# Attention opening: which engine squares and copies the second unit, and when GpSimd starts

## The chip, the cores and the metric

The kernel runs on one core of a Trainium2 chip. A core has five engines that run side by side, each with its own in-order list of instructions: PE (TensorE, matmuls), DVE (VectorE), ACT (ScalarE), POOL (GpSimd) and SP (SyncE, which here only issues DMAs). They meet through semaphores. The metric is the device time of one launch in microseconds (us), a median over runs. A profile of one execution gives the span from the first to the last instruction, each instruction's start and duration, and the PE clock that was granted.

## What is computed

Attention with root-mean-square-normalised queries and keys, and behind it a two-layer network with a leaky ReLU. q, k, v have the shape (8, 12, 448, 64): batch, heads, sequence, head dimension.

```python
def rmsnorm(x, g):
    rms = np.sqrt(np.mean(x * x, axis=-1, keepdims=True) + 1e-06)
    return x / rms * g
q_n, k_n = rmsnorm(q, g_q), rmsnorm(k, g_k)
scores = np.matmul(q_n, k_n.transpose(0, 1, 3, 2)) / np.sqrt(64)
scores = scores - np.max(scores, axis=-1, keepdims=True)
attn = np.exp(scores)
attn = attn / (np.sum(attn, axis=-1, keepdims=True) + 1e-09)
x = np.matmul(attn, v).transpose(0, 2, 1, 3).reshape(3584, 768)
h = x @ w_in                      # (768, 2048)
out = np.maximum(0.01 * h, h) @ w_out
```

## The kernel before

**Units.** The 96 heads are worked off as 24 units of four heads (three units to a batch element). A unit's q and k each lie in a tile of 128 partitions x 896 fp32 numbers: 2 pairs of heads x 7 sequence groups x 64.

**Preparation of a unit u** takes these steps, each a helper of the kernel. `load(u)` issues two DMAs on SP's queue, q and k, into a ring of three buffers, so a load waits until the unit three before has been normalised. Squares: `prep_sq` on ScalarE or `prep_sqp` on GpSimd, into tiles that share a ring of three buffers. `prep_ssq` adds up each row's 64 squares on VectorE. `prep_rinv` forms 1/rms on ScalarE with a logarithm and an exponential on a few numbers. `prep_norm` multiplies q and k by it on VectorE and writes fp16 (`n16`). `prep_tr` (through `trn` for units 1 to 3) transposes 128 x 128 blocks on PE into PSUM, and `vcopy` (VectorE) or `acopy` (ScalarE) copies them out as `qkT`; q's copy multiplies by the weights g.

**A unit's attention.** There are seven key steps t. `qk` computes a step's scores into one of two PSUM slots, `ex` takes their exponential on ScalarE into `et` (fp16). Before the first exponential one bound for the unit has to be known: `shift_max` takes the maximum of step 0 on VectorE and forms the diagonal `dg`, `shift_mm` spreads it over the partitions with one matmul, and VectorE turns it into the bias `eb`. `close(u)` sums up the exponentials on PE (`zsum_slot`), starts the next unit's exponential and second score step, multiplies with v (`pv`), and forms 1/sum on ScalarE (`zinv`: a logarithm and an exponential over 128 x 896). `xmul` multiplies the two on VectorE. `score0(u)` is a unit's score step 0 computed ahead, in two auxiliary PSUM banks.

**The order.** Under `tc.manual_schedule()` (line 576) each engine executes its instructions in the order in which the program calls the helpers. Lines 577 to 628 open unit 0, lines 650 to 681 are unit 0's seven steps with the preparation of units 1 and 2 between them, lines 683 to 708 unit 1, lines 710 to 746 unit 2, and from line 748 a loop runs over units 3 to 23; there a queue of matmul groups of the network is spread over the attention steps by a list of costs.

**GpSimd** has its own list: make constants, squares of unit 1's q (line 599), two v loads (600, 601), squares of unit 1's k (619), `gate(0)` (620), the first half of `w_in` as four DMAs (621), unit 2's squares (622), v of unit 2 (626). `gate(u)` copies one number of `n16`: it makes GpSimd, and all that is queued behind it there, wait until unit u's keys are normalised. `feed(u)` (line 629) is the loads, gate, squares and v of later units.

**Unit 0's keys** are handled in two parts: K0 is group 0, K1 groups 1 to 6; `trk` (line 608) transposes and copies a part. `warm(n, bank)` issues n matmuls of 128 x 128 whose results are not used.

The lines that fix the order around the change, before:

```python
        prep_norm(0, K0, (1,))
        tpk = aux([P, NS, P], FP16, "tp")
...
        trk(K0, vcopy)
        prep_norm(0, K1, (1,))
        qk(0, STEPS[0])
        shift_max(0)
        trk(K1, acopy)
```

Of the kernel before, what the change touches and what calls it, by code (L numbers as in the profile page):

```python
# [18 lines left out]
def kernel(  # L19
# [35 lines left out]
    def aux(shape, dtype, name):  # L55
        return psum.tile(shape, dtype, tag="aux", bufs=4, name=name)
# [30 lines left out]
    def load_w_in(n0, n):  # L87
        for a in range(2):
            for r in range(2):
                nc.gpsimd.dma_start(win16[64 * a:64 * a + 64, :, r, n0:n0 + n], win_v[a, :, :, r, n0:n0 + n])  # L90
# [7 lines left out]
    st = {}  # L98

    def rows(x, u):  # L100
        b, g = divmod(u, NQ)
        return x[b, QH * g:QH * g + QH].rearrange("(a r) (p t) d -> (r p) a (t d)", r=2, t=NS)

    def load(u, engines=None):
        raw[u] = [raws.tile([P, 2, NS, D], FP32, tag=name, name=name) for name in ("rq", "rk")]
        st[u] = {}
        for t, src, eng in zip(raw[u], (q, k), engines or (nc.sync, nc.sync)):
            eng.dma_start(t.rearrange("p a t d -> p a (t d)"), rows(src, u))

    def load_v(u):  # L110
        nc.gpsimd.dma_start(vts[u % NV].rearrange("p a t d -> p a (t d)"), rows(v, u))  # L111

    ALL = (0, NS)
# [7 lines left out]
    def buf(u, name):  # L121
        if name not in st[u]:
            shape, dtype, bufs = SHAPES[name]
            st[u][name] = prep_p.tile(shape, dtype, tag=name[:2] if bufs == 3 and name != "qkT" else name, bufs=bufs, name=name)
        return st[u][name]
# [3 lines left out]
    def prep_sq(u, c=ALL, tis=BOTH):  # L129
        for ti in tis:  # L130
            nc.scalar.activation(buf(u, f"sq{ti}")[:, :, c[0]:c[1]], raw[u][ti][:, :, c[0]:c[1]], AF.Square)  # L131

    def prep_sqp(u, tis=BOTH):
        for ti in tis:
            nc.gpsimd.tensor_tensor(buf(u, f"sq{ti}"), raw[u][ti], raw[u][ti], op=ALU.mult)
# [4 lines left out]
    def prep_ssq(u, c=ALL, tis=BOTH):  # L140
        for ti in tis:
            nc.vector.tensor_reduce(buf(u, "ssq")[:, ti, :, c[0]:c[1]], buf(u, f"sq{ti}")[:, :, c[0]:c[1]],  # L142
                                    axis=AXL.X, op=ALU.add)

    def prep_rinv(u, tis=BOTH):
        x = slice(tis[0], tis[-1] + 1)
        nc.scalar.activation(buf(u, "uu")[:, x], buf(u, "ssq")[:, x], AF.Ln, bias=eps_t, scale=1.0 / D)
        nc.scalar.activation(buf(u, "rinv")[:, x], buf(u, "uu")[:, x], AF.Exp, bias=0.0, scale=-0.5)  # L148

    def prep_norm(u, c=ALL, tis=BOTH):  # L150
        n = c[1] - c[0]
        for ti in tis:
            src = raw[u][ti]
            nc.vector.tensor_tensor(  # L154
                buf(u, "n16")[:, ti, c[0]:c[1]].rearrange("p s a d -> p a s d"), src[:, :, c[0]:c[1]],
                buf(u, "rinv")[:, ti, :, c[0]:c[1], None].broadcast_to([P, 2, n, D]), op=ALU.mult)

    def prep_tr(u, ti, copies):
        tp = aux([P, NS, P], FP16, "tp")
        for (lo, hi), copy in copies:  # L160
            for x in range(lo, hi):
                nc.tensor.transpose(tp[:, x, :], buf(u, "n16")[:, ti, x].rearrange("p a d -> p (a d)"), ident16)
            copy(buf(u, "qkT")[:, ti, lo:hi], tp[:, lo:hi], ti == 0)
# [12 lines left out]
    def slot():  # L176
        return psum.tile([P, 2, 512], FP32, tag="sT", bufs=2, name="sT")

    def score(u, t, banks):
        for r in range(2):  # L180
            for a in range(2):
                nc.tensor.matmul(banks[a][64 * r:64 * r + 64, 0:S].rearrange("p (t x) -> p t x", t=NS),  # L182
                                 kT(u, r, a, t), qT(u, r, a), start=True, stop=True)

    def qk(u, steps):
        st[u]["sT"] = []
        for t in steps:
            sT = slot()
            score(u, t, (sT[:, 0], sT[:, 1]))
            st[u]["sT"].append((t, sT))  # L190

    def ex(u):
        s = st[u]
        if "et" not in s:
            s["et"] = epool.tile([P, NS, 2, S], FP16, tag="et", name="et")
        for t, sT in s["sT"]:
            if isinstance(sT, list):
                for a in range(2):
                    nc.scalar.activation(s["et"][:, t, a], sT[a][:, 0:S], AF.Exp, bias=s["eb"], scale=1.0)
            else:  # L200
                nc.scalar.activation(s["et"][:, t], sT[:, :, 0:S], AF.Exp, bias=s["eb"], scale=1.0)  # L201
# [21 lines left out]
    def shift_bank(u):  # L223
        st[u]["pb"] = aux([P, 512], FP32, "pb")

    def shift_mm(u):
        s = st[u]
        if u > 0 and "pslot" in st[u - 1]:
            pb = st[u - 1]["pslot"][:, :, S:S + 64]
            for x in range(2):  # L230
                nc.tensor.matmul(pb[:, x], onesp, s["dg"][:, 64 * x:64 * x + 64], start=True, stop=True)
            nc.vector.tensor_reduce(s["spare"][:, 510:511], pb, axis=AXL.XY, op=ALU.max)  # L232
        else:
            if "pb" not in s:
                shift_bank(u)
            pb = s["pb"]
            nc.tensor.matmul(pb[:, 0:P], onesp, s["dg"], start=True, stop=True)
            nc.vector.tensor_reduce(s["spare"][:, 510:511], pb[:, 0:P], axis=AXL.X, op=ALU.max)
        s["eb"] = small.tile([P, 1], FP32, tag="eb", name="eb")
        nc.vector.tensor_scalar(s["eb"], s["spare"][:, 510:511], -1.0, DELTA, op0=ALU.mult, op1=ALU.add)  # L240

    def gate(u):
        nc.gpsimd.tensor_copy(gate_t, buf(u, "n16")[:, 1, NS - 1, 1, D - 1:D])
# [11 lines left out]
    def zsum_slot(u):  # L255
        s = st[u]
        s["zslot"] = slot()
        s["zt"] = [s["zslot"][:, r] for r in range(2)]
        zsum(u)
# [59 lines left out]
    def pv(u, t0=0, t1=NS):  # L319
        s = st[u]  # L320
        if t0 == 0 and "pslot" not in s:
            s["pv"] = [aux([P, 512], FP32, "pv") for r in range(2)]
        for t in range(t0, t1):
            for r in range(2):
                for a in range(2):
                    nc.tensor.matmul(s["pv"][r][64 * a:64 * a + 64, 0:S], vts[u % NV][64 * r:64 * r + 64, a, t],  # L326
                                     s["et"][64 * r:64 * r + 64, t, a], start=(t == 0), stop=(t == NS - 1))
# [241 lines left out]
    K0, K1 = (0, 1), (1, NS)  # L569
    VV = ((ALL, vcopy),)  # L570

    def warm(n, bank):
        for x in range(n):
            nc.tensor.matmul(bank[:, P:2 * P], onesp, onesp, start=True, stop=True)

    with tc.manual_schedule():
# [19 lines left out]
        nc.vector.tensor_copy(gcol, gps[:, 0:1])  # L596
        prep_ssq(0, ALL, (1,))
        prep_rinv(0, (1,))
        prep_sqp(1, (0,))
        load_v(0)  # L600
        load_v(1)
        prep_norm(0, CA, (0,))
        prep_norm(0, CB, (0,))
        prep_tr(0, 0, ((CA, acopy), (CB, acopy)))
        prep_norm(0, K0, (1,))
        tpk = aux([P, NS, P], FP16, "tp")

        def trk(c, copy):
            for x in range(*c):
                nc.tensor.transpose(tpk[:, x, :], buf(0, "n16")[:, 1, x].rearrange("p a d -> p (a d)"), ident16)  # L610
            copy(buf(0, "qkT")[:, 1, c[0]:c[1]], tpk[:, c[0]:c[1]])

        trk(K0, vcopy)
        prep_norm(0, K1, (1,))
        qk(0, STEPS[0])
        shift_max(0)
        trk(K1, acopy)
        load(3)
        prep_sqp(1, (1,))
        gate(0)  # L620
        load_w_in(0, 1024)
        prep_sqp(2)
        shift_bank(0)
        warm(12, st[0]["pb"])
        shift_mm(0)
        load_v(2)
        prep_ssq(1, ALL, (0,))

        def feed(u):
            load(u + 4)  # L630
# [4 lines left out]
        def trn(u, ti, copy):  # L635
            prep_tr(u, ti, ((ALL, copy),))
# [5 lines left out]
        def close(u):  # L642
            n = u + 1
            zsum_slot(u)
            ex(n)
            qk(n, (1,))
            pv(u)
            zinv(u)

        ex(0)  # L650
        prep_ssq(1, ALL, (1,))
        prep_rinv(1)
        prep_norm(1)
        prep_ssq(2)
        feed(0)
        load_w_in(1024, 1024)
        wb = aux([P, 512], FP32, "warm")
        qk(0, (1,))
        ex(0)
        warm(16, wb)  # L660
        qk(0, (2,))
        ex(0)
        warm(12, wb)
        qk(0, (3,))
        ex(0)
        warm(6, wb)
        qk(0, (4,))
        ex(0)
        trn(1, 0, vcopy)
        trn(1, 1, acopy)  # L670
        qk(0, (5,))
        ex(0)
        qk(0, (6,))
        ex(0)
        prep_rinv(2)
        score0(1)
        shift_max(1)
        shift_bank(1)
        warm(20, st[1]["pb"])
        shift_mm(1)  # L680
        close(0)

        prep_norm(2)
        prep_ssq(3)
# [163 lines left out]
```

The softmax here doesn't subtract the row's maximum and nothing guards it: scores larger than these inputs give would overflow.

## Time and profile before

| what | value |
|---|---|
| median of 3 runs (lowest to highest) | 432.72 us (432.71 to 432.97) |
| span of the profiled execution | 431.2 us |
| mean granted PE clock | 0.990 |
| HBM read and written | 45.61 MB, 11.01 MB |
| unit 1's exponentials start | 28.07 us |
| unit 2's exponentials start | 36.99 us |
| unit 3's first exponential | 49.20 us |

The profiled execution is one more execution of the same program; only its span is known, and what lies before its first and after its last instruction is not in it. Busy times are per engine and can overlap. In a timeline row the first number is the start in us from the beginning of the span, the second the duration; a row with xN stands for N instructions in a row, and the bracket says how long the engine had been idle and which work ended that. Instructions of one engine can overlap by about 0.1 us, as the next one is fed while the last one writes its results. What matters for this change lies in the first 50 us.

### The profile page before, as it was taken

Reading aid. Unit: us, or ns where it says so; the run is one execution under the profiler, and the core shown is the slowest. Engines: PE = TensorE matmul, PEld = TensorE weight load, DVE = VectorE, ACT = ScalarE, POOL = GpSimd, SP = SyncE. Lnnn points to the kernel's source line nnn. Section 1 sums busy time; section 2 is a strip of 40 time slices with the busy share of each in tenths; the row PEclk is TensorE's granted clock in tenths of the full one; section 3 lists DMA queues with packets and bytes.
Section 4 is the critical chain, followed back from the end, with each engine's and each line's share of the span. In section 5 each row is a group of like instructions: output and inputs, shape, how many; then the busy total and the mean of one; then the engine's idle time right before and its main releaser. Section 6 shows DMA issues by size and latency. Waiting matters only on the chain.

```text
span 431.2 us, 8844 instructions
## 1 busy us (share of the span) xinstructions
PE 409.3 (95%) x3645; PEld 211.2 (49%) x3645; DVE 273.2 (63%) x434; ACT 306.5 (71%) x466; POOL 86.6 (20%) x77
## 2 busy tenths in 40 slices
PE   7677999999989999999999999999999999999996
PEld 6545444445444544454445544454445444455553
DVE  5898656888659865487369864587359840542162
ACT  5389888757986779966986789966986757643400
POOL 2885423300002102112102102111101101010000
PEclk9699999999999999999999999999999999999999
DMA  8999993789566896578555797488572460212013
GB/s 264 198 239 252 237 254 85 143 170 221 154 104 114 194 206 161 143 128 212 156 103 136 170 209 171 130 141 194 160 109 44 118 143 16 44 38 73 2 44 103
DMA packets 66476, 62.37 MB, mean 145 GB/s; under 512 B 35716, under 2 KB 61572, under 8 KB 66436
## 3 DMA queue, kind: packets, MB, share of 16 engines
q1 hardware_dynamic: 55840, 49.62, 46.7%
q0 software_dynamic: 10272, 11.80, 17.8%
q8 instruction: 28, 0.46, 0.4%
q10 hardware_dynamic: 324, 0.39, 0.3%
q14 instruction: 12, 0.10, 0.1%
HBM read 45.61 MB, written 11.01 MB: 131 GB/s over the span
## 4 chain that ended last, share of the span: by engine, by line
PE 63%; ACT 16%; DVE 12%; issue 3%; ACTq 0%; DVEq 0%
PE hps L347 25%; ACT et L201 8%; PE ma L427 7%; PE md L427 6%; PE sT L182 5%; PE sT L326 4%; PE op L387 4%; PE mc L427 4%; DVE n L154 3%; PE mb L427 3%; ACT gt L341 3%; PE zc L269 3%; DVE ssq L142 1%; DVE sT L219 1%; ACT x L281 1%
## 5 line engine op out<-in xcount | busy, mean ns | idle before, releaser
L201 ACT ACTIVATE et<-sT,eb 128x896 f16<-128x896 f32 x166 | 158.6, 1005 | 15.6 <-PE sT L182 13.3
L347 PE MATMUL hps<-xt,win 128*128 128x448 f16 x756 | 151.0, 353 | 0.2 <-DVE xt L335 0.2
L347 PEld LDWEIGHTS <-win 128*128 128x128 f16 x756 | 70.6, 98 | 71.4 <-issue 9.9
L341 ACT ACTIVATE gt<-hps 128x448 f16<-128x448 f32 x126 | 65.7, 541 | 20.1 <-PE hps L347 19.4
L306 POOL TENSOR_TENSOR xt<-x,rz 128x896 f16<-128x896 f32 x16 | 33.5, 2092 | 150.8 <-DMA rz<-zs 49.8
L154 DVE TENSOR_TENSOR n<-rq,rinv 128x896 f16<-128x896 f32 (+2 forms) x25 | 27.5, 1102 | 48.4 <-ACT rinv L148 44.9
L182 PE MATMUL sT<-qkT 64*64 64x448 f16 x664 | 52.6, 366 | 4.8 <-ACT et L201 4.3
L142 DVE TENSOR_REDUCE ssq<-sq 128x14 f32<-128x896 f32 (+2 forms) x49 | 50.1, 1055 | 1.2 <-ACT sq L131 1.2
L427 PEld LDWEIGHTS <-sa 128*128 128x128 f16 x352 | 32.8, 98 | 26.3 <-issue 6.1
L281 ACT COPY x<-sT 128x896 f32<-128x896 f32 x19 | 17.2, 907 | 39.5 <-DVE sT L232 39.5
L111 POOL DMA_DIRECT2D vt<-in_v_dram x24 | 18.2, 760 | 114.4 <-PE sT L326 106.9
L427 PEld LDWEIGHTS <-gt 128*128 128x128 f16 x264 | 25.2, 98 | 20.3 <-issue 4.4
L219 DVE TENSOR_REDUCE sT<-sT 128x1 f32<-128x896 f32 x22 | 24.0, 1093 | 17.5 <-PE sT L182 17.5
L182 PEld LDWEIGHTS <-qkT 64*64 64x64 f16 x672 | 15.8, 104 | 39.0 <-issue 35.9
L387 PE MATMUL op<-wout,gt 128*128 128x384 f16 x192 | 34.1, 327 | 0.0
L427 PE MATMUL ma<-wout,gt 128*128 128x384 f16 x176 | 32.3, 326 | 0.1
L154 DVE TENSOR_TENSOR n<-rk,rinv 128x896 f16<-128x896 f32 (+2 forms) x25 | 30.1, 1206 | 0.0
L326 PE MATMUL sT<-et,vt 64*64 64x448 f16 x532 | 28.5, 349 | 0.3
L408 DVE TENSOR_TENSOR sa<-gt 128x512 f16<-128x512 f16 (+1 forms) x15 | 8.1, 543 | 29.6 <-ACT gt L341 29.6
L326 PEld LDWEIGHTS <-vt 64*64 64x64 f16 x672 | 20.4, 107 | 10.8 <-issue 1.1
L387 PEld LDWEIGHTS <-gt 128*128 128x128 f16 x192 | 17.7, 98 | 14.0 <-issue 3.2
L453 ACT COPY ost<-ma 128x384 f32<-128x384 f32 x11 | 5.3, 480 | 23.6 <-PE ma L427 23.6
(87 smaller groups left out, 444.9 us busy)
## 6 DMA issues: line engine op xcount, KB each, us to landing
rq<-in_q_dram SPq DMA_DIRECT2D x24, 448.0 KB, 5.0
rk<-in_k_dram SPq DMA_DIRECT2D x24, 448.0 KB, 5.9
out_dram<-ost SPq DMA_DIRECT2D x52, 192.0 KB, 3.8
rz<-zs SPq DMA_DIRECT2D x38, 224.0 KB, 3.3
vt<-in_v_dram POOLq DMA_DIRECT2D x24, 224.0 KB, 5.0
win<-in_moe_w_in_dram POOLq DMA_DIRECT2D x8, 384.0 KB, 9.4
wout<-in_moe_w_out_dram POOLq DMA_DIRECT2D x2, 1536.0 KB, 23.7
out_dram<-ost SPq DMA_DIRECT2D x4, 96.0 KB, 2.1
```

What stands on the lines that cost most here:

```text
L142: nc.vector.tensor_reduce(buf(u, "ssq")[:, ti, :, c[0]:c[1]], buf(u, f"sq{ti}")[:, :, c[0]:c[1]], axis=AXL.X, op=ALU.add)
L154: nc.vector.tensor_tensor(buf(u, "n16")[:, ti, c[0]:c[1]].rearrange("p s a d -> p a s d"), src[:, :, c[0]:c[1]], buf(u, "rinv")[:, ti, :, ...
L182: nc.tensor.matmul(banks[a][64 * r:64 * r + 64, 0:S].rearrange("p (t x) -> p t x", t=NS), kT(u, r, a, t), qT(u, r, a), start=True, stop=True)
L201: nc.scalar.activation(s["et"][:, t], sT[:, :, 0:S], AF.Exp, bias=s["eb"], scale=1.0)
L219: nc.vector.tensor_reduce(s["spare"][:, 511:512], sT[:, :, 0:S], axis=AXL.XY, op=ALU.max)
L281: nc.scalar.copy(s["x32"], s["pslot"][:, :, 0:S])
L306: eng.tensor_tensor(xts[b][:, g], s["x32"], s["rz"], op=ALU.mult)
L326: nc.tensor.matmul(s["pv"][r][64 * a:64 * a + 64, 0:S], vts[u % NV][64 * r:64 * r + 64, a, t], s["et"][64 * r:64 * r + 64, t, a], start=(t ...
L341: nc.scalar.activation(dst, src, AF.Prelu, bias=0.0, scale=1.0, alpha=0.01)
L347: nc.tensor.matmul(hps[:, 0:S], win16[:, kt // 2, kt % 2, ts(ft, P)], xt[:, kt // 2, kt % 2], start=(kt == 0), stop=(kt == KT - 1))
L387: nc.tensor.matmul(op2[:, 0:HC], gt[:, ft, ds(col(t), P)], wout16[:, ft, ds(HC * half, HC)], start=(ft == 0), stop=(ft == FT - 1))
L427: nc.tensor.matmul(bank[:, 0:HC], a[:, f], b[:, f], start=(first and f == 0), stop=(f == HF - 1), skip_group_check=not first)
```

## The change

Unit 1's squares leave GpSimd. ScalarE computes q's after unit 0's query copies and k's after the copy of K1. K1 is normalised right after K0, before K0 is transposed and copied. GpSimd's first work after the constants is `gate(0)`; behind it come v of unit 0, the first half of `w_in`, unit 2's squares, v of unit 1, v of unit 2.

In unit 0's steps, both of unit 1's sums stand behind the first bias. The second score step and its exponential move ahead of unit 1's inverse root, its normalisation and `feed(0)`. Both transposed tiles of unit 1 are copied by VectorE, q after score step 5 and k after step 6. Unit 2's sums move behind the bias of unit 1, and its inverse root behind `close(0)`. The numbers of unused matmuls change: 12 to 8 before the first bias, 6 to 12 after step 3, a new 6 after step 4, 20 to 16 before unit 1's bias.

```diff
         prep_ssq(0, ALL, (1,))
         prep_rinv(0, (1,))
-        prep_sqp(1, (0,))
-        load_v(0)
-        load_v(1)
         prep_norm(0, CA, (0,))
         prep_norm(0, CB, (0,))
         prep_tr(0, 0, ((CA, acopy), (CB, acopy)))
         prep_norm(0, K0, (1,))
+        prep_norm(0, K1, (1,))
+        prep_sq(1, ALL, (0,))
         tpk = aux([P, NS, P], FP16, "tp")
...
         trk(K0, vcopy)
-        prep_norm(0, K1, (1,))
         qk(0, STEPS[0])
         shift_max(0)
         trk(K1, acopy)
+        prep_sq(1, ALL, (1,))
         load(3)
-        prep_sqp(1, (1,))
         gate(0)
+        load_v(0)
         load_w_in(0, 1024)
         prep_sqp(2)
+        load_v(1)
         shift_bank(0)
-        warm(12, st[0]["pb"])
+        warm(8, st[0]["pb"])
         shift_mm(0)
         load_v(2)
-        prep_ssq(1, ALL, (0,))
+        prep_ssq(1)
...
         ex(0)
-        prep_ssq(1, ALL, (1,))
+        qk(0, (1,))
+        ex(0)
         prep_rinv(1)
         prep_norm(1)
-        prep_ssq(2)
         feed(0)
         load_w_in(1024, 1024)
         wb = aux([P, 512], FP32, "warm")
-        qk(0, (1,))
-        ex(0)
         warm(16, wb)
         qk(0, (2,))
         ex(0)
         warm(12, wb)
         qk(0, (3,))
         ex(0)
-        warm(6, wb)
+        warm(12, wb)
         qk(0, (4,))
         ex(0)
-        trn(1, 0, vcopy)
-        trn(1, 1, acopy)
+        warm(6, wb)
         qk(0, (5,))
         ex(0)
+        trn(1, 0, vcopy)
         qk(0, (6,))
         ex(0)
-        prep_rinv(2)
+        trn(1, 1, vcopy)
         score0(1)
         shift_max(1)
         shift_bank(1)
-        warm(20, st[1]["pb"])
+        warm(16, st[1]["pb"])
         shift_mm(1)
+        prep_ssq(2)
         close(0)
+        prep_rinv(2)
```

## The prediction

> **What bounds the kernel now.** I read the page's totals first, then busy times by stage, then the timeline of the opening engine by engine, then its chain of waits.
>
> ```profile
> PE 409.3 (95%) x3645; PEld 211.2 (49%) x3645; DVE 273.2 (63%) x434; ACT 306.5 (71%) x466; POOL 86.6 (20%) x77
> ```
>
> The page's totals: PE is busy 95% of the span, so over the whole nothing but PE can be the limit. The edit lies before 50 us, so its own stages count (columns: stage, its length, then busy us and count for PE, PEld, DVE, ACT, POOL, the granted clock, the DMA share, GB/s):
>
> ```profile
> 8.00:17.00 9.00, 4.14 (x40) 2.84 (x37) 7.67 (x8) 2.33 (x5) 7.59 (x9) 0.79 0.92 238
> 17.00:28.00 11.00, 8.88 (x113) 6.28 (x113) 9.38 (x16) 8.18 (x12) 9.59 (x11) 0.86 1.10 225
> 28.00:37.00 9.00, 6.88 (x119) 4.12 (x115) 8.31 (x15) 8.75 (x13) 7.18 (x8) 1.00 1.13 255
> ...
> 49.00:100.00 51.00, 48.62 (x459) 23.78 (x457) 38.72 (x54) 38.72 (x58) 13.31 (x11) 1.00 0.83 171
> ```
>
> From 8 to 17 us DVE works 7.67 of 9.00 us, PE 4.14, ACT 2.33. Only from 49 us is PE the limit (48.62 of 51). As every engine's order is written out by hand, a shift that reaches 49 us should reach the end. What DVE does at 8 to 17 us, from the timeline (start, duration, engine, line, operation, out<-in, count):
>
> ```profile
> 8.50 1.82 POOL L135 TENSOR_TENSOR sq<-rq 128x896 f32<-128x896 f32 x1 [7.18 <-DMA rq<-in_q_dram]
> 8.69 1.77 DVE L154 TENSOR_TENSOR n<-rk,rinv 128x128 f16<-128x128 f32 x1
> ...
> 10.92 3.48 DVE L154 TENSOR_TENSOR n<-rk,rinv 128x768 f16<-128x768 f32 x1
> ...
> 11.89 1.69 POOL L135 TENSOR_TENSOR sq<-rk 128x896 f32<-128x896 f32 x1
> ...
> 14.33 1.09 DVE L219 TENSOR_REDUCE sT<-sT 128x1 f32<-128x896 f32 x1
> ...
> 17.23 1.01 ACT L201 ACTIVATE et<-sT,eb 128x896 f16<-128x896 f32 x1 [1.12 <-DVE eb L240]
> ```
>
> The two key normalisations of unit 0 take 1.77 and 3.48 us. The same line takes 0.56 us for 384 elements (start 8.22) and 1.09 for 896 (start 27.92): 1.04 ns an element, so 128 should take 0.29 and 768 about 0.96. Each ends just after a GpSimd square: 10.46 after 10.31, 14.40 after 13.58 (plus 0.82, nearly its own length). So they stand still while GpSimd squares, 4.0 us in all, and the first exponential starts only at 17.23. Reductions are not held: the pair at 17.11 takes 2.07 beside a square.
>
> **The change, part by part.** Times are in the old span's clock; handovers are those of the same rows (PE starts 0.05 us after its releaser, VectorE 0.04 to 0.1).
>
> 1. *Unit 1's squares leave GpSimd (minus 2 x 1.7 us there) and ScalarE gets two of 0.95 (the row at 5.64).* GpSimd has nothing to run until its gate, so K0 is normalised 8.69 to 8.98 and K1, now ahead of the K0 copy, to 9.85. The score then waits for ScalarE's second query copy, ending at 10.48 unchanged: score 10.53 to 10.9 (before 11.06), maximum 10.95 to 12.03, dg to 12.42, matmul 12.47, reduction and bias to 13.24 (0.82 us after dg's end; before 1.40, because twelve fillers at half clock stood ahead; eight take 0.5 at 0.056 each and end by 11.9). First exponential at 13.27: **3.96 us earlier**. ScalarE's squares fit in its hole of 4.83 us (10.48 to 15.32): square 10.48 to 11.4, K1 copy to 12.25, square to 13.1. Without that hole they would cost 1.9. The one table load of the trace stands at 1.57, before any square, so squares beside exponentials need no other.
>
> 2. *Queued behind GpSimd's gate (9.9 instead of 14.47):* v(0), four w_in issues (0.64 each), unit 2's squares, v(1), v(2). v(0) is issued at 10.1 (before 10.26), w_in 11.0 to 13.55 (before 14.59 to 17.14), the squares 13.55 to 16.9, v(1) at 16.9 instead of 11.14. v(1) is read near 36 us, and its landing took 6.8; nothing waits. On SP the third load's k half goes at 9.9 instead of 14.47. For none of the moved issues do I charge time: between 17 and 110 us the list of waits has one DMA, 0.5 us.
>
> 3. *Unit 1's sums and normalisation:* VectorE sums 13.15 to 15.22; inverse root on ScalarE 15.27 to 15.85 between two exponentials; normalisation wants 15.95 but meets unit 2's second square, ending 16.9. The row for that is at 19.89, where a normalisation met a square ending at 20.48:
>
> ```profile
> 19.89 1.55 DVE L154 TENSOR_TENSOR n<-rq,rinv 128x896 f16<-128x896 f32 x1 [0.70 <-issue]
> ...
> 21.36 1.08 DVE L154 TENSOR_TENSOR n<-rk,rinv 128x896 f16<-128x896 f32 x1
> ```
>
> It ended 0.96 after the square, its mate at 22.44. Here likewise: 17.86 and 18.9 (3.55 earlier).
>
> The row at 10.92 is a warning: there VectorE had begun 0.97 before the square, with two v issues running, and stood anyway; by it the wait could last over v issues too (second rival). I take the row at 19.89, whose neighbours are those of here: a square, a v issue, then a gate. The Trainium skill (SBUF — State Buffer, "Who interferes with whom") says that whichever of VectorE and GpSimd issues first holds the shared ports for its whole instruction and the other waits. By that rule the 10.92 instruction should have run through, which the trace denies; here the rule would give one square's wait, 431.2 as in my sum, and the denying row 432.7.
>
> 4. *Exponentials, and both copies on VectorE:* pitch 0.89 (19.70, 20.59, 21.48). From 13.27 with the inverse root between: starts 14.16, 15.75, 16.65, 17.55, 18.45, 19.35, end 20.35. PE transposes unit 1's q after score 5 (17.7), k at 19.0 after score 6, which needs exponential 4's end (18.55), and after 18.9. Copies 0.67 and 0.62: the second ends at 20.2, though VectorE now has both; unit 2's sums (2.07), which stood ahead of them, are moved back. Score 0 of unit 1 at 20.25 instead of 25.07: **4.8 earlier**.
>
> ```profile
> 25.07 0.38 PE L182 MATMUL s<-qkT 64*64 64x448 f16 x4 [1.25 <-DVE qkT L558]
> ...
> 27.92 1.09 DVE L154 TENSOR_TENSOR n<-rq,rinv 128x896 f16<-128x896 f32 x1
> ...
> 34.49 1.15 DVE L214 TENSOR_REDUCE pm<-s 128x1 f32<-128x448 f32 x2
> ```
>
> 5. *What is late next: unit 2's inverse root, moved behind close(0).* Before, it was done at 26.46, so unit 2's normalisation followed the bias at once (27.92). Now ScalarE first does, from the bias at 23.15 (20.25 plus the old 2.90): two half exponentials to 24.35, ln and exp of the sums to 26.15 (0.92 + 0.95), inverse root to 26.7 (0.36 + 0.23). VectorE, having summed unit 2 by 25.2, stands idle until 26.75: **1.15 earlier remains of 4.8**. GpSimd's square 3k, which needs a buffer freed by those sums, runs 24.3 to 26.0, so it is clear of this normalisation; the second w_in half is issued at 26.7 as before.
>
> 6. *From there VectorE's own work is the bound:* normalisations 2.1, sums 2.07, copies 1.3 (less a 0.28 wait for PE, which is now ahead), xmul 1.15: the maximum at 33.0 instead of 34.49, 1.5 earlier, and so is unit 2's bias. ScalarE finishes unit 1's exponentials at 33.9, before the bias at 35.45. Later orders are unchanged, so 1.5 goes through to 49 us and the end.
>
> Sum: span 431.2 - 1.5 = 429.7. The three timed runs have a median of 432.72, 1.5 above the profiled span, which I take to lie around it in both kernels: **431.2 us**. Own range 430.7 to 431.8, from 0.3 either way in part 3 (where the square ends) and 0.2 to 0.3 in part 5.
>
> **The clock.** Busy PE in steps of 3.41 us, laid from the clock's changes at 6.37, 13.20 and 20.02 (then granted clock, DMA share, GB/s):
>
> ```profile
> 9.79:13.20 3.41, 0.69 (x7) 1.00 0.85 222
> 13.20:16.61 3.41, 2.15 (x23) 0.50 0.91 152
> 16.61:20.02 3.41, 3.41 (x31) 0.50 1.09 244
> ...
> 23.44:26.85 3.41, 1.99 (x28) 1.00 1.08 208
> ```
>
> 0.69 busy of 3.41 was followed by half clock, 1.99 was not, and only a full step brought it back. After the change 9.79 to 13.20 should hold some 2.5 (K0 0.2, score 0.4, K1's six transposes and fillers 1.1, matmul and next score 0.7), so I take full clock. The Trainium skill (TensorE: Matmul & The Clock Gate, "Part 4: PE-mode transpose") speaks against that: transposes do not count as busy in the same way. By it only some 1.7 would count, and with half clock to 20.0 the sum would be the first of the clock rival's two.
>
> **Rivals.**
>
> - *The clock halves at 13.2 and stays so into unit 1's first score; slower.* Place: the fillers 16, 12, 12 and 6 between unit 0's scores, then 0.107 us each (1.28 for 12), the scores 0.59. Scores 3, 4, 5 come at 16.5, 18.3, 19.5, the q transpose at 20.0, k at 20.9, score 0 of unit 1 at 22.2. It decides from 21.75 on, where all of part 6's 1.5 is used up; so half clock to 20.0 gives 433.2, within measurement. Half clock to 23.4 adds 0.25 on each block of seven transposes (0.82 for six at 14.46, 0.56 for seven at 30.52) and 0.2 on the score: 433.9, slower. For it: the half clock of before lasted 6.83 us, and a step of 2.15 did not end it. Against: 2.5 is above the 1.99 that kept the clock, and fillers at half clock stand so close that 13.2 to 16.6 would be a full step.
> - *Unit 1's normalisation also waits for the v issues queued behind the square,* to 18.4: 1.5 later, all gain gone, 432.7. For it: the row at 10.92. Against: the row at 19.89, where v was issued at 20.42 and the normalisation finished in time.
> - *Loads hide it:* the DMA share is 1.1 from 17 to 49 us; if a load became the limit the time would stay 432.7. Against: the one DMA wait of 0.5 us, and that loads are issued earlier, none later before it is needed, but for v(1).
> - *It does nothing for the held normalisations,* were GpSimd not the cause: then two added squares on ScalarE stay in its hole and the time is 432.7. The ends beside the squares speak against it.
>
> **How the numbers follow.** What a measurement here can tell from no change is 0.2%, 0.87 us: faster means under 431.85, slower over 433.59. Forecast 66%, all of it faster. Within 20%: the v issues 8, half clock to 20.0 6, loads 4, no effect 2. Slower 14%: half clock to 23.4 8, and 6 for a cost in ScalarE's new order that I have not seen. The range takes the forecast and the within cases up to 433.2, and down to 430.6; what lies above, 14%, and a little below is left out.
>
> **What would show it.** K0 and K1 normalised in 0.3 and 1.0 us; first exponential near 13.3; a normalisation of unit 1 lengthened to some 1.9 beside a square; unit 1's score 0 near 20.3; VectorE idle near 25 to 26.7; unit 2's maximum near 33.0; clock 1.0 after 13. It is wrong if the clock is 0.5 from 13 to 20, if score 0 comes after 21.75, or if what is gained at 37 us is missing at 100.

## The result, and the profile after

The change made no difference that can be measured: 432.90 us (median of 4 runs, 432.59 to 433.74) beside 432.85 for the kernel before in the same session, ratio 0.9999, 95% interval 0.9985 to 1.0013. Twelve more runs, in a later session, gave 0.9994 (0.9984 to 1.0004). The profiled execution took 432.59 us, of which the span is 430.8.

Busy time by stage of the changed kernel (columns as before the change: PE, PEld, DVE, ACT, POOL, granted clock, DMA share, GB/s):

```profile
8.00:17.00 9.00, 6.90 (x79) 4.97 (x79) 6.91 (x11) 7.63 (x11) 7.52 (x10) 0.81 1.01 267
17.00:28.00 11.00, 7.39 (x123) 4.43 (x121) 7.83 (x14) 7.93 (x12) 6.27 (x8) 1.00 1.13 237
28.00:37.00 9.00, 7.18 (x83) 3.96 (x87) 8.54 (x15) 6.05 (x10) 7.04 (x8) 0.62 1.11 224
```

From 8 to 17 us ScalarE now works 7.63 us instead of 2.33: the opening moves. But the clock, which was 1.00 from 28 to 37 us, is now 0.62 there. The opening in the timeline of the changed kernel:

```profile
8.25 1.15 DVE L154 TENSOR_TENSOR n<-rk,rinv 128x128 f16<-128x128 f32 x2
...
12.89 1.90 ACT L201 ACTIVATE et<-sT,eb 128x896 f16<-128x896 f32 x2 [0.29 <-DVE eb L240]
...
14.60 1.69 POOL L135 TENSOR_TENSOR sq<-rk 128x896 f32<-128x896 f32 x1
...
15.55 1.70 DVE L154 TENSOR_TENSOR n<-rq,rinv 128x896 f16<-128x896 f32 x1 [0.70 <-issue]
```

K0 and K1 are normalised in 1.15 us together (they took 1.77 and 3.48), and the first exponential starts at 12.89 instead of 17.23. Unit 1's normalisation takes 1.70 instead of 1.09: it ends 0.96 after the square that ends at 16.29. Further on, in the same timeline:

```profile
20.28 0.38 PE L182 MATMUL s<-qkT 64*64 64x448 f16 x4 [0.72 <-DVE qkT L560]
...
26.46 0.23 ACT L148 ACTIVATE rinv<-uu 128x28 f32<-128x28 f32 x1
...
26.77 1.09 DVE L154 TENSOR_TENSOR n<-rq,rinv 128x896 f16<-128x896 f32 x1 [1.61 <-POOL sq L135]
...
32.96 1.14 DVE L214 TENSOR_REDUCE pm<-s 128x1 f32<-128x448 f32 x2
...
34.87 2.01 PE L252 MATMUL sT<-et,ones 64*64 64x448 f16 x28
```

Unit 1's score 0 comes at 20.28 (25.07 before), unit 2's normalisation at 26.77 (27.92), its maximum at 32.96 (34.49). The bracket at 26.77 names a square that had ended at 25.93; what ended just before is unit 2's inverse root, at 26.69. The last row is the new loss. It is `zsum_slot(1)`, the sums of unit 1's exponentials, which the kernel before does in 1.52:

```profile
36.35 1.52 PE L252 MATMUL sT<-et,ones 64*64 64x448 f16 x28
```

Milestones in us (end of an instruction, in the first row its beginning), the difference to before in brackets. The second profile of the same changed kernel is the first experiment.

| milestone | before | after | after, second profile |
|---|---|---|---|
| ScalarE's square of unit 0's keys begins | 5.64 | 5.20 (-0.44) | 5.63 (-0.01) |
| unit 0's bias | 17.20 | 12.86 (-4.34) | 13.36 (-3.84) |
| unit 1's bias | 27.97 | 23.18 (-4.79) | 23.19 (-4.78) |
| unit 2's k normalised | 30.02 | 28.87 (-1.15) | 28.88 (-1.14) |
| unit 2's bias | 36.95 | 35.47 (-1.48) | 35.48 (-1.47) |
| unit 3's bias | 49.16 | 48.05 (-1.11) | 49.03 (-0.13) |
| unit 6's bias | 92.04 | 91.44 (-0.60) | 92.36 (+0.32) |
| end of the span | 431.22 | 430.81 (-0.41) | 431.68 (+0.46) |

The first row tells when unit 0's keys had landed. It differs from execution to execution: in the fourteen profiles of this document the square begins at 5.20 to 6.37 us, and what follows moves with it. So up to 1.2 us of a difference between two profiles can be this landing and not the kernel.

```profile
5.64 0.95 ACT L131 ACTIVATE sq<-rk 128x896 f32<-128x896 f32 x1 [0.51 <-DMA rk<-in_k_dram]
```

```profile
5.20 0.95 ACT L131 ACTIVATE sq<-rk 128x896 f32<-128x896 f32 x1
```

In the second profile the keys landed as before, and the gain at 37 us is the 1.5 that was worked out. In the first profile the same figure comes from two differences that cancel: the keys landed 0.44 earlier, and half clock from 12.03 to 15.44 us took 0.5 back (from the first exponential's start to unit 1's bias 10.3 us, 9.8 in the second profile).

Behind 37 us the gain is lost: 0.4 to 1.3 between the biases of units 2 and 3, about half a microsecond between 50 and 92, and 0.26 in one further place near 150 us.

### The profile page after: what moved, and what is told of

The parts are those of the page before. It is cut to its first block, busy times and chain, and to the rows that moved or that the text cites. A ratio compares the mean times of both kernels' runs of the same rounds, so it can differ in the third digit from the quotient of the medians.

```text
span 430.8 us, 8852 instructions
## 1 busy us (share of the span) xinstructions
PE 409.9 (95%) x3649; PEld 210.3 (49%) x3649; DVE 270.1 (63%) x435; ACT 307.6 (71%) x467; POOL 83.0 (19%) x75
## 4 chain that ended last, share of the span: by engine, by line
PE 65%; ACT 16%; DVE 11%; issue 4%; DMA 2%; POOL 0%; SPq 0%; DVEq 0%; ACTq 0%
PE hps L347 25%; ACT et L201 8%; PE ma L427 7%; PE sT L182 6%; PE md L427 6%; PE sT L326 4%; PE mc L427 4%; DVE n L154 4%; PE op L387 3%; PE mb L427 3%; ACT gt L341 3%; PE zc L269 3%; DMA qkT<-n 1%; DVE sT L219 1%; DVE ssq L142 1%
## 5 line engine op out<-in xcount | busy, mean ns | idle before, releaser
L154 DVE TENSOR_TENSOR n<-rk,rinv 128x896 f16<-128x896 f32 (+2 forms) x25 | 26.0, 1044 | 0.0
```

What stands on the lines that cost most here:

```text
L154: nc.vector.tensor_tensor(buf(u, "n16")[:, ti, c[0]:c[1]].rearrange("p s a d -> p a s d"), src[:, :, c[0]:c[1]], buf(u, "rinv")[:, ti, :, ...
```

## The experiments

Twelve kernels ran, in four groups, each beside runs of the kernel before on the same chip. Theories A and D, as they came to be, say: the gain is real, and half clock on PE (and perhaps one DMA) takes it back. "Fillers" are the unused matmuls of `warm`. The rivals are in the expectations.

**1. The changed kernel again**, with no edit.

> The changed kernel once more, to see what of its profile recurs. Theory A (the opening gains about 1.1 to 1.5 us at 37 us and gives it back later at places where something else ends last: the sums of unit 0 or 1 at half clock, the landing of unit 6's transposing DMA near 80 us): ratio 0.998 to 1.000; unit 2's bias 1.3 to 1.6 us earlier than before, the shift at 100 us under 0.8. Rival B (the loss in the first profile was chance, the gain normally goes through): ratio 0.996 to 0.998 and a shift of 1.1 or more at 100 us and at the end.

Ratio 0.9994 (0.9984 to 1.0004). At 92 us this execution is 0.3 later than before. Its loss sits at the same sums, now 2.83 us. Timeline row, then busy PE in steps of 3.41 us (then granted clock, DMA share, GB/s):

```profile
34.89 2.83 PE L252 MATMUL sT<-et,ones 64*64 64x448 f16 x28
```

```profile
27.66:31.07 3.41, 2.14 (x26) 1.00 1.17 191
31.07:34.48 3.41, 1.36 (x20) 1.00 1.08 242
34.48:37.90 3.42, 3.21 (x37) 0.50 1.10 258
```

PE had only 1.36 us of work from 31.07 to 34.48, and half clock followed just where the 28 sum matmuls stand. In the first profile the step with little work came earlier, while PE waited for unit 2's normalisation, and half clock lay from 29.1 to 35.9:

```profile
25.68:29.09 3.41, 1.16 (x18) 1.00 1.18 207
29.09:32.50 3.41, 2.00 (x23) 0.50 1.10 191
32.50:35.92 3.42, 3.13 (x33) 0.50 1.09 258
```

So it hit only the head of the sums there (2.01). What theory A expected came, what rival B expected did not.

**2. Fillers in PE's hole at 25.7 to 27.9 us.**

```diff
         qk(1, (2,))
         ex(1)
+        warm(32, st[1]["pb"])
         trn(2, 0, vcopy)
```

> The changed kernel with 32 unused matmuls before the transposes of unit 2's q, where PE stands idle from 25.7 to 27.9 us. If half clock from 29.1 to 35.9 us costs the 0.4 us seen between 37 and 39 us: clock 1.0 through 29 to 36, sums of unit 1 (28 matmuls) back to 1.5 us from 2.0, unit 2's second exponential 1.4 to 1.5 us earlier than before instead of 1.1. If the clock is not what loses it: no move of that exponential.

Ratio 1.0004 (0.9994 to 1.0013): nothing. The hole is full, but the step with little work came 6 us later than in the first profile, and half clock from 35.2 to 42.0:

```profile
24.94:28.35 3.41, 3.41 (x72) 1.00 0.88 195
28.35:31.76 3.41, 2.77 (x38) 1.00 1.04 152
31.76:35.17 3.41, 1.36 (x20) 1.00 1.05 216
35.17:38.58 3.41, 2.61 (x29) 0.50 1.10 252
```

The sums again took 2.83. This execution also had half clock from 11.3 to 18.1, with unit 0's scores at 14.79, 16.71 and 18.40 between fillers of 1.46 and 1.25 for twelve, and unit 1's bias at 24.47, 11.4 us after the first exponential's start where the second profile has 9.8. That is the first rival of the prediction in its place, at 1.6 us. The expectation was wrong about which hole mattered; as the sums ran at half clock, the run says nothing against the clock as the cause.

**3. Unit 2's inverse root early.**

```diff
         ex(0)
+        prep_ssq(2, ALL, (0,))
         prep_rinv(1)
...
-        def close(u):
+        def close(u, early=None):
             n = u + 1
             zsum_slot(u)
             ex(n)
+            if early:
+                prep_rinv(early)
...
-        prep_ssq(2)
-        close(0)
-        prep_rinv(2)
+        prep_ssq(2, ALL, (1,))
+        close(0, 2)
```

> The changed kernel with unit 2's inverse root before the reciprocal of unit 0 instead of behind it, the sums of its q ahead of unit 1's normalisation and of its k behind unit 1's bias. If the late inverse root is what keeps 4.8 us from arriving: unit 2 normalised near 25.0 instead of 26.8, its bias near 33.8 instead of 35.5, and 1.5 us more gain at 50 us (2.6 to 3.0 against before). Theory A expects part of it to be lost near 80 us and the end 0.5 to 1.5 us earlier than before; rival C (whatever is gained before 50 us is taken up by PE's later order or by DMAs) expects a shift at 50 us and none at the end, ratio 0.999 to 1.001; rival B expects 2.6 or more at the end, ratio 0.994.

Ratio **0.9950** (0.9938 to 0.9961). Unit 2 is normalised at 24.51 and its bias stands at 33.20, 3.75 earlier than before (0.39 of it because the keys landed earlier); unit 3's is 2.62 earlier, the end 2.4. Timeline of this kernel, one row of VectorE and one of PE:

```profile
24.51 1.09 DVE L154 TENSOR_TENSOR n<-rq,rinv 128x896 f16<-128x896 f32 x1 [0.81 <-issue]
```

```profile
32.61 2.76 PE L252 MATMUL sT<-et,ones 64*64 64x448 f16 x28
```

Rival C, that whatever is gained before 50 us is swallowed, falls: 2.62 at unit 3's bias is still 2.4 at the end, and the ratio over five runs shows a gain too. Even here the sums ran at half clock, and 1.1 us went there.

**4. VectorE scales the DMA-transposed unit behind the next sums.** From unit 6 on a DMA (line 166) transposes a unit instead of PE, and VectorE then multiplies by the weights (line 138).

```diff
-                if d == 1 and 5 <= u < NU - 1:
-                    job(prep_g, u + 1)
...
                             job(prep_ssq, u + 2, ALL, (ti,))
+                if d == 1 and 5 <= u < NU - 1:
+                    job(prep_g, u + 1)
```

> The changed kernel with VectorE's scaling of the DMA-transposed unit (line 138) behind the sums of the next unit instead of ahead of them, in every unit from 5 on. If the landing of that DMA is what took 0.5 us near 80 us: no wait for a DMA there, the shift at 100 us as large as at 75 us (1.1), the end 0.9 to 1.1 us earlier than before, ratio 0.9975. If the 0.5 us were VectorE's or PE's own order: a shift of 0.6 at 100 us as in the first profile, ratio 0.999 to 1.000.

Ratio 1.0005 (0.9993 to 1.0017). The place is this one, in the timelines of VectorE before and after:

```profile
80.62 0.56 DVE L391 COPY ost<-op 128x384 f32<-128x384 f32 x1 [0.80 <-PE op L387]
81.09 0.44 DVE L138 TENSOR_SCALAR qkT<-qkT,gcol 128x896 f16<-128x896 f16 x1
```

```profile
79.49 0.56 DVE L391 COPY ost<-op 128x384 f32<-128x384 f32 x1 [0.80 <-PE op L387]
80.49 0.45 DVE L138 TENSOR_SCALAR qkT<-qkT,gcol 128x896 f16<-128x896 f16 x1 [0.45 <-DMA qkT<-n]
```

The transposing DMA of unit 6 was issued 1.13 earlier after the change, but landed only 0.46 earlier (80.47 instead of 80.93): 6.01 us on its way instead of 5.34. With the new order no wait for it is left, and the shift is 0.11 at unit 5's bias and 0.17 at unit 6's. That alone proves little, because in this execution the DMA took 5.63 us, and VectorE's old place for it comes 5.59 us after the issue. What shows the cause is all the profiles together. In three kernels (after, 1, 11) the DMA took 5.88 to 6.01, VectorE waited 0.32 to 0.45 for it, and the stretch between the biases of units 3 and 6 took 43.28 to 43.39 us. In the eleven others it took 5.63 or less, VectorE did not wait, and the stretch took 42.80 to 42.88. As a remedy the new order was useless: the kernel lost 1.3 between 130 and 340 us, and the whole was no faster.

**5. Thirty fillers instead of twelve ahead of unit 2's bias**, in the hole that the first and second run pointed to.

```diff
         shift_bank(2)
-        warm(12, st[2]["pb"])
+        warm(30, st[2]["pb"])
```

> The changed kernel with 30 unused matmuls instead of 12 ahead of unit 2's bias (line 706 of before), where PE stands idle from 33.4 to 34.7 us. Theory D (PE, now early, idles while VectorE finishes unit 2's maximum, the clock halves, and unit 1's 28 sum matmuls take 2.0 to 2.8 us instead of 1.5): sums 1.5 us at full clock, unit 3's bias 1.3 to 1.5 us earlier than before (0.1 to 1.1 in the runs so far), the end 0.8 to 1.5 earlier, ratio 0.9965 to 0.998. Rival E (the clock is no cause; the gain is taken up by another wait at 37 to 49 us): sums shorter or not, unit 3's bias not earlier than in the runs so far, ratio 0.999 to 1.0005.

The profiled execution does what theory D says: sums 1.52, unit 3's bias 1.67 earlier than before, the end 1.13 earlier (0.25 of each because the keys landed earlier).

```profile
32.44 1.83 PE L574 MATMUL pb<-onesp 128*128 128x128 f16 x30
...
34.70 1.52 PE L252 MATMUL sT<-et,ones 64*64 64x448 f16 x28
```

The ratio over twelve runs does not: 0.9991 (0.9975 to 1.0008). The runs fall apart by their mean granted clock: the six with 0.999 or 1.000 took 431.87 to 432.92 us, the six with 0.992 or less 432.98 to 435.70. So the executions that keep the clock are the faster ones, and the fillers do not by themselves make an execution keep it.

**6. and 7. The early inverse root with 34 fillers there**, and the same with the scaling of unit 6 alone moved behind the sums.

```diff
-        warm(12, st[2]["pb"])
+        warm(34, st[2]["pb"])
```

```diff
-                if d == 1 and 5 <= u < NU - 1:
+                if d == 1 and 6 <= u < NU - 1:
                     job(prep_g, u + 1)
...
                             job(prep_ssq, u + 2, ALL, (ti,))
+                        if u == 5:
+                            job(prep_g, u + 1)
```

> The version with the early inverse root, and 34 unused matmuls instead of 12 ahead of unit 2's bias. In it the sums of unit 1 took 2.76 us at half clock. Theory D: sums 1.5, unit 3's bias 3.6 to 3.9 us earlier than before instead of 2.6, ratio 0.991 to 0.993. Rival E: bias 2.6 earlier, ratio 0.995.

> As the run before, and for unit 6 alone VectorE scales the DMA-transposed tile behind the next unit's sums instead of ahead of them. If the landing near 80 us takes up to 0.5 us there: no DMA wait of VectorE for that unit and a shift at 100 us equal to that at 60 us; against the run before 0 to 0.5 us faster. If VectorE only waits elsewhere for it: the same time, or 0.3 slower.

Ratios 0.9942 (0.9920 to 0.9963) and 0.9937 (0.9913 to 0.9960), sums 1.52 in both profiles. Unit 3's bias was 2.73 and 2.79 earlier, less than expected, with unit 1's bias a microsecond later than in experiment 3. Most of that microsecond is the landing of unit 0's keys (the square begins at 6.08 and 6.21, in experiment 3 at 5.25); half clock from 11 to 15 us took the rest, 0.25 and 0.05. The two do not differ measurably. In neither profile did unit 6's DMA land late (at 76.96, and read at 78.35, in the sixth), so the seventh tells nothing on it.

**8. Unit 1's squares back on GpSimd**, all else as changed.

```diff
-        prep_sq(1, ALL, (0,))
+        prep_sqp(1, (0,))
...
-        prep_sq(1, ALL, (1,))
+        prep_sqp(1, (1,))
```

> The changed kernel with unit 1's squares back on GpSimd ahead of its gate, all else as changed. If GpSimd's squares are what holds the key normalisations: K0 and K1 each end within 0.2 us after a square plus own length, K1 near 12 us instead of 9.4, and unit 0's first bias near 15.0 to 15.7 instead of 12.9. If the old K1 place behind the K0 copy was the cause: K0 and K1 take 0.3 and 1.0 us and the bias stays near 12.9. The end: what is lost before 28 us falls through later waits of VectorE for unit 2's inverse root; ratio 1.001 to 1.007.

Ratio 1.0058 (1.0039 to 1.0077). GpSimd and then VectorE in this kernel's timeline:

```profile
8.87 1.98 POOL L135 TENSOR_TENSOR sq<-rq 128x896 f32<-128x896 f32 x1 [7.56 <-DMA rq<-in_q_dram]
10.81 1.72 POOL L135 TENSOR_TENSOR sq<-rk 128x896 f32<-128x896 f32 x1
```

```profile
9.23 4.12 DVE L154 TENSOR_TENSOR n<-rk,rinv 128x128 f16<-128x128 f32 x2
```

K0 ended at 11.00, 0.15 after the first square, K1 at 13.35, 0.81 after the second; together 4.12 us instead of 1.15. The place of K1 in the order is the same as in the changed kernel, so the squares are the cause. Unit 0's bias came at 16.52, later than expected, but in this execution the keys landed 0.98 later than in the changed kernel's first profile (the square begins at 6.18); counted from that square, the bias is 2.68 later.

**9. and 10. Fillers in every hole before 35 us**, in the changed kernel and in the version with the early inverse root (there without the 32 of experiment 2, and 34 for 30).

```diff
-        prep_tr(0, 0, ((CA, acopy), (CB, acopy)))
+        def awarm(dst, src, scaled=False):
+            acopy(dst, src, scaled)
+            warm(12, wbank)
+
+        prep_tr(0, 0, ((CA, awarm), (CB, acopy)))
...
         trk(K0, vcopy)
+        warm(8, wbank)
...
-        warm(8, st[0]["pb"])
+        warm(16, st[0]["pb"])
...
+        warm(32, st[1]["pb"])
         trn(2, 0, vcopy)
...
-        warm(12, st[2]["pb"])
+        warm(30, st[2]["pb"])
```

> The changed kernel with unused matmuls in every hole of PE before 35 us: 12 more between unit 0's query transposes, 8 before its first score, 16 instead of 8 before its bias, 32 before unit 2's q transposes, 30 instead of 12 before unit 2's bias. Theory D: what the opening gains was lost to half clock whose place differs from execution to execution, so with no half clock before 430 us in any of them the gain of 1.1 to 1.7 us of the full-clock executions becomes the rule: mean granted clock 0.998 or more in nearly all, unit 3's bias 1.4 to 1.7 us earlier than before, ratio 0.9955 to 0.9975, narrower than the 4 us spread of the run with 30 fillers alone. Rival F (the executions at full clock were fast for another reason): clock 0.998 and a ratio of 0.999 to 1.000.

> The early inverse root with 34 unused matmuls ahead of unit 2's bias and the fillers of the opening. Theory D: clock 0.998 or more, unit 0's first bias at 12.9 to 13.4 in all executions, ratio 0.991 to 0.994. Rival F: no better than the early inverse root alone, 0.995.

The changed kernel with the fillers: ratio 0.9981 (0.9970 to 0.9992), short of what was expected, with the clock at 0.996 in eleven runs of twelve, which is one half-clock step somewhere (3.41 us at half of 431 us lower the mean by 0.004). In the one profiled execution, the slowest of the twelve, unit 0's bias came at 14.87, 2.0 later than in the changed kernel's first profile: 1.17 of it because the keys landed later (the square begins at 6.37), and 0.84 because half clock from 10.6 to 14.0 met the longer rows of fillers (sixteen took 1.80, 0.11 us each). The version with the early inverse root: ratio **0.9931** (0.9913 to 0.9949), 430.11 us beside 433.70, clock 0.999 or more in five of six runs, unit 3's bias 3.70 earlier, the end 3.34 (0.30 of each from the landing). It beats both kernels.

**11. The one part undone: unit 2's sums and inverse root back in their old places.**

```diff
         prep_norm(1)
+        prep_ssq(2)
         feed(0)
...
         trn(1, 1, vcopy)
+        prep_rinv(2)
         score0(1)
...
-        prep_ssq(2)
         close(0)
-        prep_rinv(2)
```

> The changed kernel with one part undone: unit 2's sums again right behind unit 1's normalisation and its inverse root again ahead of unit 1's score 0, all else as changed. By rows: sums 18.25 to 20.3, copies of unit 1 to 21.6, score 0 near 21.65 (20.3 as changed), unit 1's bias near 24.5 (23.2), but unit 2 normalised at once, 24.6 instead of 26.8. If moving those two cost what part 5 of the prediction counted: unit 2's bias near 33.2 (35.5 as changed, 36.95 before), 2 us better than the change, ratio 0.994 to 0.997. Rival G (the copies and score 0 behind the sums lose as much as the early inverse root gains): unit 2's bias 35.0 to 36.0, ratio 0.999 to 1.001.

Ratio **0.9958** (0.9941 to 0.9975). VectorE in this kernel's timeline:

```profile
18.27 2.07 DVE L142 TENSOR_REDUCE ssq<-sq 128x14 f32<-128x896 f32 x2
...
24.42 1.09 DVE L154 TENSOR_TENSOR n<-rq,rinv 128x896 f16<-128x896 f32 x1
...
30.07 0.62 DVE L560 COPY qkT<-tp 128x896 f16<-128x896 f16 x1 [0.90 <-PE tp L162]
```

Unit 1's bias is at 24.47, 1.3 later than as changed, but unit 2 is normalised at once, 24.42 instead of 26.77. Its bias stands at 34.13 (-2.82 against before); the 0.9 short of expectation is VectorE's wait at 30.07 for the k transposes, which PE does only after a score step that waits for a slot. Rival G falls: moving these two items cost more than it gave.

**12. The control: fillers in the kernel before.**

```diff
         qk(0, STEPS[0])
+        warm(28, wbank)
         shift_max(0)
```

> The kernel before with 28 unused matmuls behind unit 0's first score, in PE's hole from 11.4 to 14.5 us, as a control of the clock. If before too loses by its half clock from 13.2 to 20.0: clock nearer 1.0, unit 0's bias 0.3 to 0.6 us earlier, ratio 0.9985 to 0.9995; then part of what fillers gained in the other runs is open to the old order as well. If before is bound by VectorE there whatever the clock: ratio 0.9995 to 1.0005.

Ratio 1.0043 (1.0026 to 1.0060): slower, which neither side expected. In its profile unit 0's bias is 1.0 earlier (0.4 of it from the landing of the keys), but half clock lies at 11.0 to 14.4, 24.6 to 28.0 and 34.9 to 38.3. The twenty old fillers ahead of unit 1's bias then took 2.32 us instead of 1.29, and the gain was gone. So fillers are no safe lever here, and this run leaves open what before would take at full clock.

**All fourteen profiles together.** The stretch between the biases of units 2 and 3 holds the same instructions in the same order in all of them. Its length, worked out from the ends of the two bias rows, against the half clock that follows unit 2's bias:

| kernel | half clock after unit 2's bias, us | the 28 sums, us | stretch, us |
|---|---|---|---|
| before; 5; 6; 7; 10; 11 | 0 | 1.52 | 12.20 to 12.21 |
| 9 | 0.19 | 1.89 | 12.46 |
| after | 0.45 | 2.01 | 12.59 |
| 12 | 0.77 | 2.17 | 12.75 |
| 8 | 0.81 | 2.19 | 12.76 |
| 3 | 1.97 | 2.76 | 13.34 |
| 1 | 2.41 | 2.83 | 13.55 |
| 4 | 2.87 | 2.83 | 13.77 |
| 2 | 5.24 | 2.83 | 14.94 |

Without half clock the stretch is the same to 0.01. With it the stretch grows as the half clock does. The sums begin 0.60 us ahead of the end of the bias row, so the second column leaves out part of what acts on them; counted from the start of the sums, a microsecond of half clock costs 0.3 to 0.5 us. That settles the loss between 37 and 49 us in the profiled executions.

In the executions without a profile half clock is seen only in the mean clock. None of the sixteen executions of the changed kernel (the four of the result, twelve of experiment 1) has a mean above 0.995, so each had half clock somewhere. But their spans do not follow the mean: 429.8 us at 0.990, 431.7 at 0.995. Where the half clock lay in them, and what it cost them, is not shown.

**The 0.26 near 150 us** goes with the change itself. Between the biases of units 10 and 11 the eleven kernels in which ScalarE squares unit 1 take 14.92 or 14.93 us; the three in which GpSimd does (before, 8, 12) take 14.65 or 14.66, with the same instructions in that stretch. In the changed kernel ScalarE's copy at line 281 begins 0.37 after the end of VectorE's reduction at line 232, which releases it in the kernel before after 0.09. Why two squares at 10 us do this at 155 us is not shown.

## What was right in the prediction, and what failed

The forecast was a gain, 431.2 us with 430.7 to 431.8 around it; what came was no change, 432.90. That this lies below the 433.2 up to which the range was drawn is luck: the range took in four other cases, and none of them is what happened as a whole. One of the prediction's own signs of being wrong was met: of the 1.5 us gained at 37 us the first profile had 0.6 left at 92, the second nothing.

**Parts 1 to 6 up to unit 2's bias were right.** First exponential 13.39 in the second profile (13.27 was forecast; 12.89 in the first, where the keys landed 0.44 earlier). From unit 1 on the first profile agrees to a tenth: score 0 of unit 1 at 20.28 (20.25), unit 1's bias 23.18 (23.15), unit 2's normalisation 26.77 (26.75), its maximum 32.96 (33.0), its bias 35.47 (35.45). There the agreement is partly luck, the early landing against half clock at 12 to 15 us; the second profile has the same times to 0.02 without either. Experiment 8 shows the cause of the first gain, GpSimd's squares. The second rival, a wait over the v issues too, did not come: unit 1's normalisation ended 0.96 after the square with a v issue (16.22) beside it.

**The late inverse root (part 5) was the right diagnosis.** It keeps 1.15 of 4.8, and experiment 11 shows that without moving it the same change is 0.42% faster than before.

**The step that failed is the end of part 6, "Later orders are unchanged, so 1.5 goes through to 49 us and the end".** The orders are unchanged, but not PE's clock under them. Because VectorE's chain from the late normalisation to unit 2's bias did not shrink, while PE's and ScalarE's work for unit 1 came earlier, PE was left with 1.16 or 1.36 us of work in a step of 3.41, and the clock was halved on the sums right behind. The prediction had looked at the clock in the opening alone, where it reckoned 9.79 to 13.20; the stage that the change itself thins out, 25 to 35 us, was not reckoned, though part 5 had VectorE idle there and PE waiting for it.

In the opening, too, "full clock" held only by where the steps lay. Its 2.5 us of work fits the steps that lie nearly as assumed (2.66 at 10.59 to 14.00 in the second profile, full clock behind it). But the steps lie elsewhere in each execution: in the first profile the one from 8.61 to 12.02 held 1.65, and half clock followed. So the clock rival did come in the opening in some executions: 0.5 us in the first profile, where it lasted 3.4 us, and 1.6 in experiment 2, where it lasted the 6.8 that the rival priced at 2.0. That transposes might not count as busy, which the prediction weighed, does not fit these runs: in the second profile the step from 27.66 to 31.07 held 2.14 us, of which 0.99 were two rows of transposes, and full clock followed; the next step held 1.36 without a transpose, and half clock followed.

No rival named the half clock behind unit 2's bias, which took 0.4 and 1.3 us in the two profiles of the changed kernel.

**Smaller terms.** The landing of unit 6's transposing DMA took about 0.5 us of what was left, in both profiles of the changed kernel. The loads rival had the kind of wait, and was played down because the list of waits before showed one of 0.5 us. That one stands at unit 8 (107.64), where a wait of 1.45 after the change cost nothing; unit 6's is not in the list, because it landed 0.16 before it was read, and so little slack does not show there. The 0.26 near 150 us, which goes with ScalarE's two squares, was charged nothing either. And what lies around the span is 1.78 us in the profiled execution after, where 1.5 was taken from a median of other executions: the forecast should have been 431.5 from the same sum.

## What to carry to other kernels

When a change removes work or waits ahead of the limiting chain, ask which engine then stands idle, and whether that idleness lowers PE's clock for what comes next: busy time per 3.41 us step of PE, after the change, over the whole stretch up to where PE is the limit, belongs in the sum. When an item is moved back to let something pass, follow what it feeds as far as what it passed: here the moved sums and inverse root passed 4.8 us of gain and let 1.15 through. An added row of unused matmuls is a gamble: twenty of them take 1.3 us at full clock and 2.3 at half. And before two profiles are compared to a tenth, look when the first loads landed in each: here that alone was up to 1.2 us.

## What the runs showed of the hardware

- The half-clock stretches start on a grid of 3.41 us that lies differently in each execution: in the profiles their starts, taken modulo 3.413, are 2.96, 1.78, 0.35, 1.04, 0.61 and so on. The Trainium skill (TensorE: Matmul & The Clock Gate, "What's actually happening") says that the activity window runs freely and does not start with the kernel; these runs agree. The executions of one kernel differ by 4 us (431.87 to 435.70 in experiment 5, the slower six at a lower mean clock).
- Half clock does not need PE to be idle for long. Up to 50 us it began twenty times in the fourteen profiles, after steps with 0.56 to 1.86 busy microseconds of 3.41. No step with 1.91 or more was followed by it, and two steps with less kept the full clock (1.56 at 24.25 to 27.66 in experiment 1, 1.72 at 23.96 to 27.38 in experiment 5), while one with 1.83 did not (28.35 to 31.76 in experiment 3). So busy time as the profile counts it gives no sharp threshold. The same page ("HAM oscillation — how this bites in real kernels") gives as a rule no idle gap over 3.4 us. Here the longest single gap of PE from 8 to 50 us was 3.0, and in experiment 3 half clock came with no gap over 1.3; the measurement decides, and the rule is too mild here.
- One and the same transposing DMA, unit 6's, took 4.1 to 6.0 us from issue to landing in the fourteen profiles.
